# Hash-bucketed attention and two expert layers on one core: turned tiles leave PSUM as an fp16 pair

## The chip, the cores and the metric

One core of a Trainium2 chip. The metric is the device time of one launch in microseconds. Before the change: median 802.08 us of 3 runs (801.53 to 806.88).

## What is computed

Attention for 2 batches, 8 heads, 768 positions and head size 64, in which a query sees only the keys that fall in its own bucket (six sign bits of a projection), then two feed-forward layers on the 1536 x 512 result:

```python
mask = q_bucket[:, :, :, None] == k_bucket[:, :, None, :]
scores = scale * np.matmul(q, k.transpose(0, 1, 3, 2))
scores = np.where(mask, scores, -1000000000.0)
attn = np.exp(scores - np.max(scores, axis=-1, keepdims=True))
attn = attn / (np.sum(attn, axis=-1, keepdims=True) + 1e-09)
x = np.matmul(attn, v)            # then regrouped to (1536, 512)
h = x @ w_in;  x = (h / (1 + np.exp(-h))) @ w_out
h = x @ w_in2; x = (h - np.tanh(h)) @ w_out2
```

## The kernel before

The attention works on tiles of 128 queries against all 768 keys of a head: 6 tiles for each of 16 heads, 96 in all, numbered i. Tiles 0 to 47 are the first batch. For each tile, `scores` (L237) makes the masked scores in PSUM (tile `ps`, two buffers in the first batch), `soft_max` (L248) copies them to SBUF on VectorE and takes the row maximum (L257), `soft_exp` (L261) takes the exponential in place on ScalarE. The product with V needs the weights with keys on the partitions, and there are two ways to turn them:

- Even tiles of the first batch and all of the second: ScalarE rounds to fp16 (`soft_hi`, L299), GpSimd takes the remainder in fp16 (`soft_lo`, L306), and a transposing DMA on SyncE's queue (L308) brings both into a tile `pt`, of which the pool has four buffers. `pv` (L311) then makes 18 products of 128x65: for each of 6 key blocks rounded weights times rounded V (L325), rounded weights times V's remainder (L326), and weights' remainder times rounded V (L327). Column 64 of V is one, so that column 64 of the result is the row sum.
- Odd tiles of the first batch ("direct", L273; here called turned tiles, 24 of them): `turn_p` (L276) transposes on TensorE in fp32 (L285, three blocks for each of two PSUM banks `psm`), copies one bank out on ScalarE (L290) and the other on VectorE (L288) into the spare half of the tile's own SBUF buffer, and `pv` makes 6 fp32 products with V as it was loaded (L321). The row sums come from an accumulator of the exponential (L269), and `denom` takes them up in an operation of its own (L336).

`psm` has three buffers in the first batch; hashes (L172), transposes and the expert layers share them. V of a batch is loaded to `vr` (L194, a buffer that has a single copy and is later used by an accumulator of the expert layers), its row maxima are taken on VectorE (L202), and `prep_v2` writes it as `v16` (ScalarE, L232) and `v16l` (VectorE, L233).

The loop over steps s issues scores of tile s, the turn or the transposing DMA of tile s-2 and the product of tile s-6. Between the batches stand 13 steps without scores. The weights of the expert layers are converted from step 33 on, and from step 61 the expert products (L547 into the hidden layer, L571 out of it) are mixed with the second batch's attention; some 430 us of expert products alone follow. The code's order is not the order of the program: a scheduler reorders the instructions of each engine by priorities and by when it expects buffers free, and each engine then executes its own list in order.

Of the kernel before, what the change touches and what calls it, by code (L numbers as in the profile page):

```python
# [7 lines left out]
F32 = mybir.dt.float32  # L8
F32R = mybir.dt.float32r
F16 = mybir.dt.float16  # L10
I32 = mybir.dt.int32
ACTF = mybir.ActivationFunctionType
ALU = mybir.AluOpType
# [5 lines left out]
PSC = 2.0 ** 11  # L19
# [30 lines left out]
def lsh_attention_moe_kernel(  # L50
# [12 lines left out]
    nc = tc.nc  # L63
    B, H, _, _, S = qkT.shape
    DM, NT = outT.shape
    KD = DM // 128
    D = DM // H
    DFF = w_out1.shape[0]
    NQ = S // 128
    HS = S // 2  # L70
# [8 lines left out]
    sm = ctx.enter_context(tc.tile_pool(name="sm", bufs=4))  # L79
# [24 lines left out]
    def bank():  # L104
        turn[0] += 1
        pool = ps_more[0] if ps_more and turn[0] % ps_turn[1] < ps_turn[0] else ps_m
        return pool.tile([128, 512], F32, tag="m", name="psm")


    def attention(pools, vraw, extra, xw):  # L110
# [6 lines left out]
        xa = [x.rearrange("p a b -> p (a b)") for x in xa]  # L117
        xset = (xa[0][:, 0:S], xa[0][:, S:2 * S], xa[1][:, 0:S], xa[1][:, S:2 * S])

        hlx, vf, vmxs = {}, {}, {}  # L120
        raw, ops, vv, pso, sums, xt, hilo, ptile, pexp, pss, dens = {}, {}, {}, {}, {}, {}, {}, {}, {}, {}, {}

        def load_qk(n):
            b, h = divmod(n, H)
# [66 lines left out]
        def load_v(b):  # L191
            vr = vraw.tile([128, NQ, DM], F32, tag="acc", name="vr")
            for t in range(0, NQ, 2):
                nc.sync.dma_start(out=vr[:, t:t + 2, :],  # L194
                                  in_=v[b, t * 128:(t + 2) * 128].rearrange("(t p) d -> p t d", p=128))
            return vr
# [31 lines left out]
        @early  # L228
        def prep_v2(b, vr, t):
            v16, v16l, vsc = vv[b]  # L230
            src = vr[:, t, :].rearrange("p (h d) -> p h d", h=H)
            nc.scalar.activation(out=v16[:, t, :, 0:D], in_=src, func=ACTF.Copy, scale=vsc)  # L232
            nc.vector.scalar_tensor_tensor(v16l[:, t, :, 0:D], src, vsc, v16[:, t, :, 0:D],  # L233
                                           op0=ALU.mult, op1=ALU.subtract)
            vf[b] = vr

        def scores(i):  # L237
            n, t = divmod(i, NQ)
# [22 lines left out]
        def soft_exp(i):  # L261
            n, t = divmod(i, NQ)
            p, m = pexp[i]
            bi = sm.tile([128, 1], F32, tag="bi", name="bi")
            nc.scalar.activation(out=bi, in_=m, func=ACTF.Copy, scale=-0.125, bias=LN_PSC)
            if direct(i):
                if n not in sums:
                    sums[n] = sm.tile([128, NQ], F32, tag="sums", name="sums")
                nc.scalar.activation(out=p, in_=p, func=ACTF.Exp, scale=0.125, bias=bi, accum_out=sums[n][:, t:t + 1])  # L269
                return  # L270
            nc.scalar.activation(out=p, in_=p, func=ACTF.Exp, scale=0.125, bias=bi)  # L271

        def direct(i):  # L273
            return i < H * NQ and i % 2 == 1

        def turn_p(i):  # L276
            p, _ = pexp.pop(i)
            pt = hlx.pop(i) if i in hlx else wk.tile([128, 2, S], F16, tag="hl", name="ptf")
            pt = pt.rearrange("p a s -> p (a s)").bitcast(F32).rearrange("p (a q) -> p a q", a=NQ)
            w = NQ // 2  # L280
            for u in range(2):
                ps = bank()
                for x in range(w):
                    kt = u * w + x
                    nc.tensor.transpose(ps[:, x * 128:(x + 1) * 128], p[:, kt * 128:(kt + 1) * 128], ident)  # L285
                dst = pt[:, u * w:(u + 1) * w, :].rearrange("p a q -> p (a q)")
                if u:
                    nc.vector.tensor_copy(dst, ps[:, 0:HS])  # L288
                else:
                    nc.scalar.copy(dst, ps[:, 0:HS])  # L290
            ptile[i] = pt

        def soft_hi(i):
# [17 lines left out]
        def pv(i):  # L311
            n, t = divmod(i, NQ)
            b, h = divmod(n, H)
            v16, v16l, _ = vv[b]
            pt = ptile.pop(i)
            if t == 0:
                pso[n] = ps_v.tile([128, NQ, D + 1], F32, tag="o", name="pso")
            o = pso[n][:, t, :]
            if direct(i):
                for kt in range(NQ):  # L320
                    nc.tensor.matmul(out=o[:, 0:D], lhsT=pt[:, kt, :], rhs=vf[b][:, kt, h * D:(h + 1) * D],  # L321
                                     start=(kt == 0), stop=(kt == NQ - 1))
                return
            for kt in range(NQ):
                nc.tensor.matmul(out=o, lhsT=pt[:, kt, :], rhs=v16[:, kt, h, :], start=(kt == 0), stop=False)  # L325
                nc.tensor.matmul(out=o, lhsT=pt[:, kt, :], rhs=v16l[:, kt, h, :], start=False, stop=False)  # L326
                nc.tensor.matmul(out=o, lhsT=pt[:, NQ + kt, :], rhs=v16[:, kt, h, :], start=False,  # L327
                                 stop=(kt == NQ - 1))

        def denom(n):  # L330
            vsc = vv[n // H][2]
            den = sm.tile([128, NQ], F32, tag="den", name="den")
            c = 2 if n < H else 1
            nc.vector.tensor_scalar(den[:, 0:NQ:c], pso[n][:, 0:NQ:c, D], 1e-9 * PSC, vsc, op0=ALU.add, op1=ALU.mult)
            if c > 1:
                nc.vector.tensor_scalar(den[:, 1:NQ:2], sums.pop(n)[:, 1:NQ:2], 1e-9 * PSC, None, op0=ALU.add)  # L336
            nc.vector.reciprocal(den, den)
            dens[n] = den

# [43 lines left out]
        vr = load_v(0)  # L383
# [4 lines left out]
        def at(s):  # L388
            b, r = divmod(s, per + gap)
            return b * per + r if s >= 0 and b < B and r < per else None  # L390

        for s in range(B * (per + gap)):
            evs, late = late, []
            i, i1, i2, j, j1, j3 = (at(s - x) for x in (0, 1, 2, LAG, LAG + 1, LAG + 2))
# [4 lines left out]
            if i2 is not None and direct(i2):  # L399
                turn_p(i2)  # L400
# [5 lines left out]
            if j is not None:  # L406
                pv(j)
# [3 lines left out]
            if i is not None:  # L411
                n, t = divmod(i, NQ)
# [4 lines left out]
            if i is not None:  # L417
                soft_exp(i)
            if j is not None and j % NQ == NQ - 1:
                denom(j // NQ)  # L420
            late += [e2 for e2 in [e() for e in evs] if e2 is not None]
            if i is not None:
                if i % per < 2:
                    for u in range(3):
                        prep_vm(n // H, vr, 3 * (i % per) + u)
                if i % per == 1:
                    prep_v0(n // H, vr)
                    prep_v1(n // H, vr)
                if 2 <= i % per < 4:
                    for u in range(3):  # L430
                        prep_v2(n // H, vr, 3 * (i % per - 2) + u)
                if prep[0] < NHEAD and prep[0] <= limit(n):
                    if prep[1] == 0:
                        split_a(prep[0])
                    elif prep[1] == 1:
                        split_b(prep[0])
                    prep[1] += 1
                    if prep[1] == 3:
                        prep[:] = [prep[0] + 1, 0]
                while nextr < NHEAD and nextr <= (limit(n) + 1 if n < H - 1 else n + (2 if t >= 3 else 1)):  # L440
                    load_qk(nextr)
                    nextr += 1
                if n + 1 < NHEAD:
                    if (n + 1) % H == 0 and t == 0:
                        vr = load_v((n + 1) // H)
# [206 lines left out]
    with ExitStack() as es:  # L652
# [5 lines left out]
        ps_s2 = [es2.enter_context(tc.tile_pool(name="ps_s2", bufs=1, space=PSUM))]  # L658
        pools.append(ps_s2)
        attn = attention(pools, pB[5], pB[3], pB[0])  # L660
        half = NTL // 2 + LAG + GAP
        pre = None
# [87 lines left out]
```

## Time and profile before

| | |
|---|---|
| median of 3 runs | 802.08 us |
| the profiled execution | 797.22 us |
| its span (first to last instruction) | 795.4 us |
| TensorE busy | 744.3 us, 94% |
| VectorE busy | 539.5 us, 68% |
| ScalarE busy | 430.7 us, 54% |
| GpSimd busy | 308.2 us, 39% |
| mean granted TensorE clock | 0.981 |

PE is TensorE, PEld its weight load, DVE VectorE, ACT ScalarE, POOL GpSimd, SP SyncE; a q behind the name means the engine's queue of DMA and control instructions. "Idle before" is the time that the engine stood still just ahead of an instruction, and the arrow names what ended it. Durations of neighbouring instructions overlap at their ends, so an engine's throughput is read from start to start. The granted clock is a share of 2.4 GHz; 0.5 is 1.2 GHz.

### The profile page before, as it was taken

The numbers are of one execution on the slowest core, as the hardware profiler recorded it, in microseconds if no ns is written. First come the engines' busy times: TensorE is split into PE (matmuls) and PEld (weight loads), VectorE is DVE, ScalarE is ACT, GpSimd is POOL, SyncE is SP. The second block draws the span as 40 slices with busy tenths as digits, with TensorE's granted clock in tenths as the row PEclk, the third lists the DMA queues.
The fourth block names the chain that finished last, engine by engine and source line by source line (L and its number), as shares of the span: only waits on it lengthen the run. The fifth ranks groups of instructions, "written<-read, shape, count | busy, mean of one in ns | idle before, by whom it ended". The sixth has DMA issues, their size and how long they took to land.

```text
span 795.4 us, 14025 instructions
## 1 busy us (share of the span) xinstructions
PE 744.3 (94%) x5348; PEld 717.6 (90%) x5348; DVE 539.5 (68%) x1013; ACT 430.7 (54%) x821; POOL 308.2 (39%) x214
## 2 busy tenths in 40 slices
PE   4799997789999998897999999999999999999998
PEld 3789986779988888797999999999999999999998
DVE  6768789698768868777452543998658576584342
ACT  4768878677778769747353441653424334252130
POOL 4455646555766757656355420223011110111000
PEclk8699999989999999999999999999999999999999
DMA  7676587779998996984233320234122220210102
GB/s 256 140 131 131 126 188 194 187 199 191 239 219 204 227 235 136 252 208 140 80 107 106 96 91 1 81 105 130 40 70 60 73 79 30 80 53 1 50 30 80
DMA packets 138878, 100.38 MB, mean 126 GB/s; under 512 B 115870, under 2 KB 118174, under 8 KB 138810
## 3 DMA queue, kind: packets, MB, share of 16 engines
q1 hardware_dynamic: 137712, 97.54, 48.9%
q10 hardware_dynamic: 1098, 1.94, 1.0%
q8 instruction: 42, 0.69, 0.4%
q14 instruction: 26, 0.21, 0.1%
HBM read 57.95 MB, written 11.53 MB: 87 GB/s over the span
## 4 chain that ended last, share of the span: by engine, by line
PE 64%; DMA 7%; ACT 2%; issue 2%; DVE 2%; POOL 1%; SPq 0%; POOLq 0%; ACTq 0%; DVEq 0%
PE psm L571 32%; PE psm L547 29%; DMA pt<-hl 6%; PE ps L244 2%; DMA w<-in_w_out_dram 1%; PE pso L325 1%; POOL hl L306 1%; ACT p L271 1%; PE psm L172 0%; PE pso L327 0%; PE pso L326 0%; DVE cv L525 0%; POOL wl L516 0%; ACT hl L299 0%; ACT cv L523 0%
## 5 line engine op out<-in xcount | busy, mean ns | idle before, releaser
L547 PE MATMUL psm<-xh,wh 128*128 128x384 f32 x512 | 174.9, 342 | 2.1 <-DVE gl L559 1.8
L547 PE MATMUL psm<-xl,wh 128*128 128x384 f32 x512 | 172.9, 338 | 2.1 <-DVE xl L359 2.1
L516 POOL TENSOR_TENSOR wl<-wa,wh 128x512 fp32r<-128x512 f32 x64 | 83.5, 1305 | 232.1 <-ACT wh L515 232.0
L571 PE MATMUL psm<-gh,wh 128*128 128x384 f32 x512 | 172.1, 337 | 0.2 <-DVE gl L559 0.2
L547 PE MATMUL psm<-xh,wl 128*128 128x384 f32 x512 | 171.5, 337 | 0.0
L571 PE MATMUL psm<-gl,wh 128*128 128x384 f32 x512 | 171.2, 334 | 0.0
L571 PE MATMUL psm<-gh,wl 128*128 128x384 f32 x512 | 169.4, 335 | 0.0
L306 POOL TENSOR_TENSOR hl<-p,hl 128x768 f16<-128x768 f32 x72 | 119.8, 1665 | 98.4 <-ACT hl L299 90.7
L257 DVE TENSOR_SCALAR_CACHE_REDUCE p<-ps 128x768 f32<-128x768 f32 x96 | 90.8, 952 | 29.8 <-PE ps L244 24.6
L547 PEld LDWEIGHTS psm<-xh,wh 128*128 128x128 f32 x512 | 97.0, 189 | 2.5 <-DVE gl L559 2.0
L547 PEld LDWEIGHTS psm<-xl,wh 128*128 128x128 f32 x512 | 96.9, 189 | 2.6 <-DVE xl L359 2.6
L244 PE MATMUL ps<-k,q 128*128 128x384 f32 x336 | 82.0, 368 | 17.0 <-DVE p L257 13.8
L547 PEld LDWEIGHTS psm<-xh,wl 128*128 128x128 f32 x512 | 96.7, 189 | 0.1
L571 PEld LDWEIGHTS psm<-gh,wh 128*128 128x128 f32 x512 | 96.1, 188 | 0.6 <-DVE gl L559 0.6
L583 DVE TENSOR_TENSOR acc<-acc,psm 128x384 f32<-128x384 f32 x96 | 52.0, 551 | 65.2 <-PE psm L571 64.6
L571 PEld LDWEIGHTS psm<-gl,wh 128*128 128x128 f32 x512 | 96.2, 188 | 0.0
L571 PEld LDWEIGHTS psm<-gh,wl 128*128 128x128 f32 x512 | 95.8, 188 | 0.0
L559 DVE TENSOR_TENSOR gl<-psm,gh 128x384 fp32r<-128x384 f32 x128 | 70.6, 554 | 29.6 <-ACT gh L558 29.5
L558 ACT CAST gh<-psm 128x384 fp32r<-128x384 f32 x128 | 61.1, 479 | 50.9 <-DVE psm L557 34.4
L244 PEld LDWEIGHTS ps<-k,q 128*128 128x128 f32 x336 | 59.8, 199 | 21.6 <-DVE p L257 17.2
L515 ACT CAST wh<-wa 128x512 fp32r<-128x512 f32 x64 | 39.5, 617 | 60.0 <-DVE wa L514 59.5
L556 ACT ACTIVATE th<-psm 128x384 f32<-128x384 f32 x64 | 31.5, 492 | 71.9 <-PE psm L547 71.7
(99 smaller groups left out, 1298.2 us busy)
## 6 DMA issues: line engine op xcount, KB each, us to landing
w<-in_w_in_dram SPq DMA_DIRECT2D x32, 512.0 KB
w<-in_w_out_dram SPq DMA_DIRECT2D x32, 512.0 KB
r<-in_qkT_dram SPq DMA_DIRECT2D x15, 768.0 KB
wi<-wa SPq DMA_DIRECT2D x16, 256.0 KB
wo<-wa SPq DMA_DIRECT2D x16, 256.0 KB
w<-wi SPq DMA_DIRECT2D x16, 256.0 KB
w<-wo SPq DMA_DIRECT2D x16, 256.0 KB
vr<-in_v_dram SPq DMA_DIRECT2D x6, 512.0 KB
```

What stands on the lines that cost most here:

```text
L244: nc.tensor.matmul(out=ps[:, u, 0:HS], lhsT=a[:, t * 128:(t + 1) * 128], rhs=c[:, u * HS:(u + 1) * HS], start=(j == 0), stop=(j == 1))
L257: nc.vector.tensor_scalar(p.rearrange("p (c s) -> p c s", c=2), pss.pop(i)[:, :, 0:HS], FLOOR, None, op0=ALU.max, op1=ALU.max, accum_out=m)
L271: nc.scalar.activation(out=p, in_=p, func=ACTF.Exp, scale=0.125, bias=bi)
L306: nc.gpsimd.tensor_tensor(hl[:, 1, :], p, hl[:, 0, :], op=ALU.subtract)
L515: nc.scalar.copy(hh, s)
L516: nc.gpsimd.tensor_tensor(ll, s, hh.bitcast(F32), op=ALU.subtract)
L547: nc.tensor.matmul(out=ps, lhsT=a[:, k, fs], rhs=b_[blk][:, k, :], start=(k == 0 and j == 0), stop=(k == KD - 1 and j == 2))
L556: nc.scalar.activation(out=th, in_=ps, func=ACTF.Tanh)
L558: nc.scalar.copy(gh[:, f, :], ps)
L559: nc.vector.tensor_tensor(gl[:, f, :], ps, gh[:, f, :].bitcast(F32), op=ALU.subtract)
L571: nc.tensor.matmul(out=ps, lhsT=a[:, f, ds], rhs=b_[:, f, :], start=(f == 0 and j == 0), stop=(f == F - 1 and j == 2))
L583: nc.vector.tensor_tensor(ac, ac, ps, op=ALU.add)
```

## The change

Turned tiles stay turned on TensorE, but leave PSUM as the DMA's tiles arrive: rounded to fp16 by ScalarE (both banks), with the remainder taken by VectorE from the same bank into the same `pt` tile, which now comes from the pool of four. All tiles take the 18 fp16 products; the fp32 product, the accumulated sums and the reference to `vr` behind `prep_v2` go.

```diff
         def soft_exp(i):
...
-            if direct(i):
-                if n not in sums:
-                    sums[n] = sm.tile([128, NQ], F32, tag="sums", name="sums")
-                nc.scalar.activation(out=p, in_=p, func=ACTF.Exp, scale=0.125, bias=bi, accum_out=sums[n][:, t:t + 1])
-                return
             nc.scalar.activation(out=p, in_=p, func=ACTF.Exp, scale=0.125, bias=bi)
...
         def turn_p(i):
             p, _ = pexp.pop(i)
-            pt = hlx.pop(i) if i in hlx else wk.tile([128, 2, S], F16, tag="hl", name="ptf")
-            pt = pt.rearrange("p a s -> p (a s)").bitcast(F32).rearrange("p (a q) -> p a q", a=NQ)
+            pt = pt_p.tile([128, 2 * NQ, 128], F16, tag="pt", name="pt")
...
-                dst = pt[:, u * w:(u + 1) * w, :].rearrange("p a q -> p (a q)")
-                if u:
-                    nc.vector.tensor_copy(dst, ps[:, 0:HS])
-                else:
-                    nc.scalar.copy(dst, ps[:, 0:HS])
+                hi, lo = (pt[:, x + u * w:x + (u + 1) * w, :].rearrange("p a q -> p (a q)") for x in (0, NQ))
+                nc.scalar.copy(hi, ps[:, 0:HS])
+                nc.vector.tensor_tensor(lo, ps[:, 0:HS], hi, op=ALU.subtract)
             ptile[i] = pt
...
         def pv(i):
...
-            if direct(i):
-                for kt in range(NQ):
-                    nc.tensor.matmul(out=o[:, 0:D], lhsT=pt[:, kt, :], rhs=vf[b][:, kt, h * D:(h + 1) * D],
-                                     start=(kt == 0), stop=(kt == NQ - 1))
-                return
...
         def denom(n):
...
-            c = 2 if n < H else 1
-            nc.vector.tensor_scalar(den[:, 0:NQ:c], pso[n][:, 0:NQ:c, D], 1e-9 * PSC, vsc, op0=ALU.add, op1=ALU.mult)
-            if c > 1:
-                nc.vector.tensor_scalar(den[:, 1:NQ:2], sums.pop(n)[:, 1:NQ:2], 1e-9 * PSC, None, op0=ALU.add)
+            nc.vector.tensor_scalar(den, pso[n][:, :, D], 1e-9 * PSC, vsc, op0=ALU.add, op1=ALU.mult)
```

The lines move: the transposes of `turn_p` are L278 in the changed kernel, its cast L280, its subtraction L281, the scores L243, the row maximum of the softmax L256, the transposing DMA L299, the three products L311, L312 and L313.

The scheduler's order changes with it in three places.

SyncE's list, from the sixth row on, before and then after. `vr` is the fp32 slab of V, `r` the q and k of a head, `hl` the pair of an even tile:

```order
L134 DMA r<-in_qkT_dram 128x1536
L308 DMA_TRANSPOSE pt<-hl 128x12x128 x3
L134 DMA r<-in_qkT_dram 128x1536
L308 DMA_TRANSPOSE pt<-hl 128x12x128 x3
L134 DMA r<-in_qkT_dram 128x1536
L308 DMA_TRANSPOSE pt<-hl 128x12x128 x4
```

```order
L194 DMA vr<-in_v_dram 128x2x512 x3
L134 DMA r<-in_qkT_dram 128x1536
L299 DMA_TRANSPOSE pt<-hl 128x12x128 x3
L134 DMA r<-in_qkT_dram 128x1536
L299 DMA_TRANSPOSE pt<-hl 128x12x128 x3
L134 DMA r<-in_qkT_dram 128x1536
```

The load of the second batch's V, which stood behind the 24th transpose of the list, stands behind the second.

VectorE's list behind the preparation of the first batch's V, before and then after:

```order
L257 TENSOR_SCALAR p,mx<-ps 128x768 x2
L288 COPY p<-psm 128x384
L336 TENSOR_SCALAR den<-sums 128x3
L288 COPY p<-psm 128x384
L257 TENSOR_SCALAR p,mx<-ps 128x768 x2
L185 TENSOR_SCALAR hb<-psm,cst_sb 82x384 x2
```

```order
L281 TENSOR_TENSOR pt<-psm,pt 128x384 x2
L256 TENSOR_SCALAR p,mx<-ps 128x768
L202 TENSOR_REDUCE vm<-vr 128x1 x2
L281 TENSOR_TENSOR pt<-psm,pt 128x384
L256 TENSOR_SCALAR p,mx<-ps 128x768
L202 TENSOR_REDUCE vm<-vr 128x1 x2
L281 TENSOR_TENSOR pt<-psm,pt 128x384 x2
L202 TENSOR_REDUCE vm<-vr 128x1 x2
L256 TENSOR_SCALAR p,mx<-ps 128x768
```

Where single copies stood there are pairs of subtractions, and the row maxima of the second batch's V stand among the first batch's seventh to ninth softmax.

TensorE's list around the last scores of the first batch (`ps_1884` before, `ps_2176` after), before and then after. The names `pt` with a number are tiles of turned weights, `p` with a number the weights ahead of the turn:

```order
L244 MATMUL ps_1884<-k1_1255,q1_1253 128x384 x2
L244 MATMUL ps_1884<-k2_1256,q2_1254 128x384 x2
L351 MATMUL psm_1761<-cst_sb_69,xt_1474 128x128 x3
L172 MATMUL psm_1802<-q1_1721,hw_128 82x384
L172 MATMUL psm_1802<-k1_1723,hw_128 82x384
L172 MATMUL psm_1802<-q2_1722,hw_128 82x384
```

```order
L243 MATMUL ps_2176<-k1_1432,q1_1430 128x384 x2
L243 MATMUL ps_2176<-k2_1433,q2_1431 128x384 x2
L243 MATMUL ps_2373<-k1_1986,q1_1984 128x384 x2
L278 MATMUL psm_1917<-cst_sb_69,p_1841 128x128 x3
L278 MATMUL psm_2002<-cst_sb_69,p_1923 128x128 x3
L278 MATMUL psm_2008<-cst_sb_69,p_1923 128x128 x3
L311 LDWEIGHTS pt_1813
```

Behind these scores eight tiles' products are still to come in the list before, and twelve in the list after; in the middle of the batch scores stand six to seven tiles ahead of the products before, and seven to twelve after.

## Rows read from the trace of the kernel before

**Rows 1.** Groups by line: names, shapes, count | busy us, mean ns | idle before.

```profile
L321 PE MATMUL pso<-vr,p 128*128 128x64 f32 x264 | 35.0, 281 | 0.0
...
L336 DVE TENSOR_SCALAR den<-sums 128x3 f32<-128x3 f32 x8 | 5.3, 659 | 1.0 <-ACT p L269 1.0
L269 ACT ACTIVATION_READ_ACCUMULATOR p<-p,bi 128x1 f32 x24 | 4.5, 188 | 0.0
...
L356 ACT CAST xh<-psm 128x384 fp32r<-128x384 f32 x8 | 3.7, 471 | 0.0
...
L321 PE MATMUL pso<-vr,ptf 128*128 128x64 f32 x24 | 3.0, 274 | 0.0
```

**Rows 2.** Busy time by stage: stretch, PE, PEld, DVE, ACT, POOL, granted clock, DMA share, GB/s.

```profile
60.00:100.00 40.00, 39.82 (x417) 37.64 (x418) 32.07 (x66) 34.29 (x71) 23.99 (x14) 1.00 0.59 129
100.00:139.00 39.00, 32.72 (x321) 29.93 (x320) 33.56 (x64) 31.25 (x63) 21.34 (x13) 0.96 0.78 192
20.00:139.00 119.00, 106.72 (x1008) 98.58 (x1006) 93.80 (x182) 93.59 (x187) 65.75 (x39) 0.93 0.68 152
139.00:153.00 14.00, 12.89 (x138) 12.15 (x137) 8.06 (x19) 9.11 (x18) 7.69 (x8) 1.00 0.63 148
153.00:190.00 37.00, 30.08 (x231) 26.31 (x231) 32.98 (x67) 29.63 (x55) 20.72 (x14) 0.91 0.88 218
190.00:364.00 174.00, 157.99 (x1499) 146.12 (x1497) 132.65 (x260) 126.46 (x222) 111.67 (x73) 1.00 0.95 213
364.00:795.00 431.00, 427.83 (x2454) 427.39 (x2454) 259.37 (x466) 163.10 (x328) 93.43 (x75) 1.00 0.23 70
...
20.00:40.00 20.00, 15.76 (x100) 14.06 (x99) 15.87 (x28) 14.71 (x28) 9.99 (x6) 0.69 0.65 139
120.00:140.00 20.00, 15.52 (x139) 14.00 (x139) 17.82 (x32) 17.26 (x37) 13.85 (x9) 0.91 0.72 186
140.00:160.00 20.00, 15.16 (x146) 13.34 (x144) 13.74 (x30) 13.80 (x24) 11.10 (x9) 0.97 0.71 191
```

**Rows 3.** Timeline of TensorE, 65 to 68 us: start, us, instruction.

```profile
65.92 0.20 PE L325 MATMUL pso<-v,pt 128*128 128x65 f16 x1
...
66.47 1.53 PE L321 MATMUL pso<-vr,p 128*128 128x64 f32 x12
67.84 0.19 PE L325 MATMUL pso<-v,pt 128*128 128x65 f16 x1
```

**Rows 4.** Timeline of ScalarE at 66 us.

```profile
66.22 0.46 ACT L290 COPY p<-psm 128x384 f32<-128x384 f32 x1
66.58 0.84 ACT L299 CAST hl<-p 128x768 f16<-128x768 f32 x1
```

**Rows 5.** Timeline of VectorE, 155 to 162 us.

```profile
155.94 1.28 DVE L202 TENSOR_REDUCE vm<-vr 128x1 f32<-128x512 f32 x2 [0.79 <-DMA vr<-in_v_dram]
...
158.01 1.28 DVE L202 TENSOR_REDUCE vm<-vr 128x1 f32<-128x512 f32 x2
...
159.79 1.27 DVE L202 TENSOR_REDUCE vm<-vr 128x1 f32<-128x512 f32 x2
160.98 1.02 DVE L359 TENSOR_TENSOR xl<-psm,xh 128x384 fp32r<-128x384 f32 x2
161.91 0.95 DVE L257 TENSOR_SCALAR_CACHE_REDUCE p<-ps 128x768 f32<-128x768 f32 x1
```

**Rows 6.** Timeline of TensorE, 150 to 162 us; in brackets its idle time before.

```profile
150.19 0.20 PE L325 MATMUL pso<-v,pt 128*128 128x65 f16 x1 [1.11 <-DMA pt<-hl]
...
161.59 0.69 PE L547 MATMUL psm<-xl,wh 128*128 128x384 f32 x1 [2.07 <-DVE xl L359]
```

**Rows 7.** Timeline of SyncE's queue at 146 us.

```profile
146.49 1.51 SPq L308 DMA_TRANSPOSE pt<-hl  x1
```

**Rows 8.** The chain that ended last: start, us, what.

```profile
180.84 7.62 DMA pt<-hl
...
284.71 9.51 DMA pt<-hl
```

More of the change, by code (lines that the diff above doesn't have):

```diff
@@ L118, in attention @@
         xset = (xa[0][:, 0:S], xa[0][:, S:2 * S], xa[1][:, 0:S], xa[1][:, S:2 * S])
-        hlx, vf, vmxs = {}, {}, {}
-        raw, ops, vv, pso, sums, xt, hilo, ptile, pexp, pss, dens = {}, {}, {}, {}, {}, {}, {}, {}, {}, {}, {}
+        hlx, vmxs = {}, {}
+        raw, ops, vv, pso, xt, hilo, ptile, pexp, pss, dens = {}, {}, {}, {}, {}, {}, {}, {}, {}, {}
         def load_qk(n):
@@ L234, in prep_v2 @@
                                            op0=ALU.mult, op1=ALU.subtract)
-            vf[b] = vr
         def scores(i):
```

## Prediction

> **What bounds the kernel now.** I read the table of stages first, then the groups by line, then the timelines of TensorE, VectorE and SyncE at the places the change touches, and last the chain of waits. The profiled execution took 797.22 us (a span of 795.4 and 1.8 around it); the median shown is 802.08, so the sum below is made on 797.22 and carried over as a share.
>
> The change lies in the attention of the first batch, roughly the stretch from 20 to 153 us, and it frees a load that now falls just behind it. In 20 to 139, where that batch's scores are taken, TensorE is busy 106.72 of 119 us, VectorE 93.80 and ScalarE 93.59; in 139 to 153, the drain of its last value products, 12.89, 8.06 and 9.11 of 14 [rows 2]. Together that is 119.6 us of TensorE in 133, or 0.90, against 101.9 and 102.7. So TensorE is the fullest engine, but not by much. The reader is to see two more things there. From 60 to 100 it is TensorE alone (39.82 of 40). From 100 to 139, where the expert weights begin to be converted beside the attention, VectorE has 33.56 of 39 and TensorE 32.72. Behind 364 only expert products run, and TensorE is busy 427.83 of 431: nothing there can move except by starting earlier or later.
>
> **The change part by part.** There are 24 turned tiles in the first batch (i odd, below 48).
>
> *The value product.* Before, a turned tile takes six fp32 products at L321, which the trace shows as 12 records each; the groups add up to 264 and 24 [rows 1]. At full clock the 12 records start at 66.47 and the next product starts at 67.84: 1.37 us. The 18 fp16 records ahead of them start at 65.92: 0.55 us [rows 3]. The change puts the second in place of the first: 24 x 0.82 = 19.7 us less of TensorE, so 99.9 in that stretch.
>
> *Leaving PSUM.* Before, one half-tile is copied by ScalarE and one by VectorE. Now ScalarE casts both halves to fp16 and VectorE subtracts both. Copies on ScalarE start 0.36 us apart from what follows (66.22 to 66.58) [rows 4], a cast from PSUM of that size lasts as long (471 ns by its group [rows 1]); so ScalarE gets 24 x 0.36 = 8.6 us, less 24 accumulator reads of 188 ns (4.5 us, [rows 1]), and 106.8 in all. Two subtractions of this form on VectorE take 0.93 us (160.98 to 161.91) [rows 5], 0.47 each; one copy goes, two subtractions come, so 24 x 0.47 = 11.3 us. The eight operations on the sums at L336 go (5.3 us [rows 1]); the denominators' other operation takes six columns for three, which I cost at nothing, beside a VectorE sum of over 100 us. The remainder needs the rounded part, so a half-tile's bank is held for both operations in turn, and TensorE waits for the second where it waited for one.
>
> *The load of V.* The fp32 slab of V was read by L321 until the last turned tile; now only prep_v2 reads it. The second batch's load of V therefore moves on SyncE from behind the last fp32 product to behind the second transpose, and its six row maxima on VectorE from the start of the second batch to the first's seventh softmax, as the order shows. They take 1.28 + 1.28 + 1.27 us at 155.94 to 161.06 [rows 5]; that 4 us goes into the first stretch. VectorE there: 101.9 + 11.3 - 5.3 + 4.1 = 112.0 us. The three DMAs are queued ahead of a q/k load and the third transpose on SyncE, and the maxima ahead of three softmaxes on VectorE; if the slab lands late they all wait. TensorE is busy 15.76 of 20 there at a granted 0.69 [rows 2], so up to about 4 us of that is free; I charge nothing more.
>
> *The sum of the first stretch.* The fullest engine is now VectorE with 112.0, with ScalarE 106.8 and TensorE 99.9 beside it. How full can it get? TensorE got 0.90 of the stage; VectorE got 0.86 from 100 to 139 and 0.80 from 60 to 100 [rows 2]. At 0.90 the stage takes 124.5 us (8.5 less), at 0.80 140 (7 more). I take 0.86, since those are the rows in which VectorE is the fullest engine: 130.2, or 2.8 us less.
>
> *Behind it.* VectorE did the three pairs of maxima between 155.94 and 161.06, right ahead of the remainder of x at 160.98; the expert product that needs it waited 2.07 us, till 161.59 [rows 5, 6]. TensorE is busy 30.08 of 37 us from 153 to 190 [rows 2], so the gain lies between nothing and 6.9 us; I take 3.0, near the 3.8 us taken off VectorE. Later stages keep their work; their order changes a little, and from 190 to 364 TensorE has 16 us idle that can go either way by some 4 us.
>
> Sum: -2.8 - 3.0 = -5.8 us, 797.2 to 791.4, or -0.73%; on the median 802.08 that is **796.2 us**. Most of the 19.7 us is lost again: the stage ends with VectorE where TensorE ended it.
>
> **A rule that speaks against the change.** With 99.9 of 130 us, TensorE would be as loosely filled as in 120 to 140 and 140 to 160, where it was busy 15.52 and 15.16 of 20; the granted clock there was 0.91 and 0.97, mostly its upper level (2.4 GHz) with stretches of the lower (1.2) [rows 2]. The Trainium skill, TensorE: Matmul & The Clock Gate, section "HAM oscillation — how this bites in real kernels", says that products which come in bursts with waits between them lose the upper clock again and again. By that rule more of the stretch would run at 1.2 GHz than these rows show, and the last rival below has its price; by the rows nothing is added.
>
> **The rivals.**
>
> *The drain and the stage stay tight.* VectorE reaches the 0.90 that TensorE had, and the whole idle time from 153 to 190 goes: -8.5 - 6.9 = -15.4 us, 786.7 on the median. For it: the scores now run further ahead of the products, as the order shows, so VectorE seldom has nothing to take. Against it: no row shows VectorE above 0.89 (32.98 of 37) for as long.
>
> *The pt buffers decide (slower).* All 48 tiles now share four pt buffers that 24 had, so a transpose by DMA or a cast may begin only when the product four tiles earlier is done. The order shows what that does: twelve products are left when the last score of the batch is issued, where eight were. With four buffers twelve products are three rounds, and I price a round at the landing of a transpose and three products of 0.55 us. A transpose in the first batch was issued at 146.49 and its product started at 150.19 after a wait for it: 3.7 us [rows 6, 7], and the drain takes 16 us, as the sum above has room for. In the second batch transposes on the chain took 7.62 and 9.51 us [rows 8]. At 9.51 the drain takes 33.5 us, 17.4 more: 802.08 - 5.8 + 17.4, about 813.7. The gain is gone from a landing time of 5.6 us on, and slower by 1% from 8.3. For it: DMA share in the first batch 0.59 to 0.78, and a load added. Against it: the wait at 150.19 was 1.11 us, and from 60 to 100 TensorE waited for next to nothing [rows 2, 6].
>
> *The clock.* If the first stretch ran at a granted 0.69, as from 20 to 40 [rows 2], in place of 0.93, TensorE's 99.9 us become 134.6 and it is the bound again: 149.6 at 0.90, 16.6 more than before, less the 3.0 behind it: about 815.7. Against it are the two rows of the same fill, 0.91 and 0.97.
>
> **How the numbers follow.** About 1% is what a measurement of this kernel can tell from no change. Forecast 0.42 (its own range 790 to 803; most of it within 1%, 0.03 beyond at either side), tight stage 0.38, pt buffers 0.15 (at 7.62 us it would still be within 1%, so 0.04 of it), clock 0.05. Faster by over 1% (below 794.1): 0.37 + 0.03 = 0.40. Within 1%: 0.36 + 0.01 + 0.04 + 0.01 = 0.42. Slower: 0.03 + 0.11 + 0.04 = 0.18. The range reaches from the tight stage, 785, to 811, which leaves out the far end of the two slower cases.
>
> **What the next profile would show.** Right: 576 records at each of the three fp16 product lines (six for each of 96 tiles) and none in fp32; 48 casts near 0.47 us and 48 subtractions near 0.55; the maxima of the second batch before 60 us; VectorE at about 112 us in a first stretch of about 130; the first expert products some 5 to 6 us earlier. Wrong: a first stretch of 125 or less (the tight stage), long waits of the products for DMA pt in the drain (the buffers), a granted clock well below 0.9 there, or TensorE records from 190 to 364 with other idle time than 16 us, which the sum holds constant.

## The result and the profile after

The changed kernel takes 791.38 us (median of 4 runs, 789.84 to 792.62) against 802.24: a ratio of 0.9857, interval 0.982 to 0.9894. A second set gave 792.17 us and 0.9871 (0.9844 to 0.9898). So it is faster by 1.3 to 1.4%, some 11 us, where 5.8 us were forecast; the time lies inside the range.

The profile of after, by stage (columns as in [rows 2]):

```profile
20.00:139.00 119.00, 97.21 (x1103) 83.54 (x1101) 93.02 (x193) 93.60 (x180) 64.97 (x38) 0.92 0.72 149
139.00:153.00 14.00, 10.13 (x123) 8.94 (x124) 11.75 (x22) 9.20 (x18) 5.36 (x4) 0.76 0.98 242
153.00:190.00 37.00, 32.38 (x302) 30.00 (x301) 34.30 (x66) 31.50 (x60) 21.97 (x16) 0.95 0.71 164
190.00:364.00 174.00, 165.41 (x1525) 151.48 (x1524) 138.62 (x273) 131.92 (x235) 116.27 (x77) 0.99 1.01 219
364.00:795.00 431.00, 419.88 (x2422) 418.97 (x2420) 254.07 (x455) 158.08 (x318) 91.97 (x72) 1.00 0.22 70
```

Against [rows 2] the first stretch has 9.5 us less of TensorE in the same 119 us: the work went, and idle time came in its place. VectorE, which was to reach 112 us in 130, has 104.8 in 133. The surprise is in 190 to 364, which the sum held constant: TensorE is busy 165.41 of 174 where it was 157.99.

The page's busy line of after, and the groups by line that answer to [rows 1]:

```profile
PE 733.6 (93%) x5492; PEld 700.0 (89%) x5492; DVE 544.4 (69%) x1029; ACT 433.1 (55%) x821; POOL 309.5 (39%) x214
```

```profile
L311 PE MATMUL pso<-v,pt 128*128 128x65 f16 x576 | 70.9, 200 | 15.4 <-DMA pt<-hl 15.3
...
L281 DVE TENSOR_TENSOR pt<-psm,pt 128x384 f16<-128x384 f32 x48 | 25.3, 548 | 4.7 <-ACT pt L280 4.6
...
L280 ACT CAST pt<-psm 128x384 f16<-128x384 f32 x48 | 21.9, 475 | 17.1 <-PE psm L278 15.8 <-PE pso L313 0.8 <-issue 0.3
```

The change does what it says: 576 records at each fp16 line, 48 casts of 475 ns, 48 subtractions of 548 ns.

To place the gain I use one measure for every trace: the **work left** at a time, which is TensorE's busy time in stretches of 2 us times their granted clock, summed from there to the end. Two kernels with the same work left at 190 us are equally far. What the rest takes beyond it is the **loss behind 190** (idle time and lower clock).

```
work left (us) at         20     60    100    140    190   span   loss behind 190
before                 724.8  695.8  656.0  624.0  584.3  795.4   21.1
before, second trace   724.4  694.6  654.8  623.2  583.6  803.0   29.4
after                  710.4  683.4  652.9  621.6  583.7  789.4   15.7
after, second trace    711.9  684.6  652.4  622.0  585.6  792.6   17.0
late_v                 710.7  680.8  643.7  616.2  580.6  797.8   27.2
own_pt                 709.1  683.3  647.3  619.1  586.5  800.4   23.9
mid_11                 709.9  677.6  645.1  617.1  573.0  781.3   18.3
mid_11, second trace   710.3  677.9  644.3  615.8  571.7  779.1   17.4
mid_23                 713.2  680.5  646.4  618.3  575.8  778.6   12.8
mid_35                 714.7  681.7  644.8  620.4  584.3  794.5   20.2
max_held               708.0  677.7  645.7  617.2  585.1  801.9   26.8
mid_11_every4          703.5  675.4  648.1  623.1  591.5  794.7   13.2
double_sub             715.1  692.8  656.0  629.0  593.3  800.3   17.0
```

The measure is good to some 3 us: the ten traces from after on that have the same TensorE instructions (all but mid_11_every4) are equally far at 20 us and give 708.0 to 715.1 there. So the main readings are also made **by records**: the records still to come, each at its median step from start to start (177 ns for scores, 173 for expert products, 112 for fp32 transposes and fp32 value products, 29 for fp16 value products). That gives 608.9 and 608.5 us left at 140 us before and 607.7 and 607.1 after, and at 190 us 572.5 and 572.1 before and 571.9 and 573.4 after.

At 20 us the change has 13.4 us less ahead of it (means of two traces; 19.7 by records). At 190 us nothing is left of that, by either count, and the whole measured gain arises behind 190, where both kernels have the same instructions to execute. Two things are to be explained: who took those 13 to 20 us, and why the rest loses less. The names after the first four are the experiments below.

### The profile page after: what moved, and what is told of

Its sections match the earlier page's. It is cut to its first block, busy times and chain, and to the rows that moved or that the text cites. A ratio compares the mean times of both kernels' runs of the same rounds, so it can differ in the third digit from the quotient of the medians.

```text
span 789.4 us, 14334 instructions
## 1 busy us (share of the span) xinstructions
PE 733.6 (93%) x5492; PEld 700.0 (89%) x5492; DVE 544.4 (69%) x1029; ACT 433.1 (55%) x821; POOL 309.5 (39%) x214
## 4 chain that ended last, share of the span: by engine, by line
PE 55%; DMA 2%; ACT 1%; DVE 0%; issue 0%; POOL 0%; ACTq 0%; DVEq 0%
PE psm L554 28%; PE psm L530 26%; DMA pt<-hl 1%; DMA w<-wi 1%; PE ps L243 0%; ACT xh L577 0%; ACT p L265 0%; POOL hl L297 0%; PE pso L311 0%; POOL wl L485 0%; ACT wh L484 0%; ACT th L536 0%; PE pso L312 0%; PE pso L313 0%; ACT hl L290 0%
## 5 line engine op out<-in xcount | busy, mean ns | idle before, releaser
L256 DVE TENSOR_SCALAR_CACHE_REDUCE p<-ps 128x768 f32<-128x768 f32 x96 | 90.8, 952 | 29.7 <-PE ps L243 20.0
L243 PE MATMUL ps<-k,q 128*128 128x384 f32 x336 | 82.9, 372 | 15.9 <-DVE p L256 9.0
L265 ACT ACTIVATE p<-p,bi 128x768 f32<-128x768 f32 x96 | 89.0, 939 | 2.9
L311 PE MATMUL pso<-v,pt 128*128 128x65 f16 x576 | 70.9, 200 | 15.4 <-DMA pt<-hl 15.3
L311 PEld LDWEIGHTS <-pt 128*128 128x128 f16 x576 | 55.3, 101 | 27.2 <-DMA pt<-hl 17.4
```

The lines of the kernel that those rows point to most:

```text
L243: nc.tensor.matmul(out=ps[:, u, 0:HS], lhsT=a[:, t * 128:(t + 1) * 128], rhs=c[:, u * HS:(u + 1) * HS], start=(j == 0), stop=(j == 1))
L256: nc.vector.tensor_scalar(p.rearrange("p (c s) -> p c s", c=2), pss.pop(i)[:, :, 0:HS], FLOOR, None, op0=ALU.max, op1=ALU.max, accum_out=m)
```

## The experiments

**The two kernels again.**

> The kernel before, unchanged, for a second trace: its first profiled execution took 797.22 us where the timed runs took 801.5 to 806.9. Expected ratio 1.00. If the 4 to 5 us come and go between executions, this trace is longer than 797 in one stretch, and that stretch says which part of the measured gain of 10.9 us the two profiles (797.22 and 791.22, 6.0 apart) don't show. If the trace is again at 797, the profile itself makes the kernel faster.

> The changed kernel, unchanged, for a second trace and a tighter interval: ratio 0.984 to 0.988, 790 to 792 us. Every theory expects the same; if TensorE's idle time behind 190 us is again near 14 us where the kernel before had 19.6, the gain behind 190 is no accident of one execution.

Before: 804.74 us (ratio 0.9997, 0.9967 to 1.0026), its trace 803.0 us long. The execution that the forecast was made on (797.22 us) is below every timed run of this kernel (the lowest of three sets is 797.54). Its second trace is level with it to about 1 us up to 190 us, and loses 8 us behind:

```profile
190.00:364.00 174.00, 159.52 (x1455) 147.90 (x1454) 129.38 (x253) 122.04 (x211) 108.89 (x70) 0.97 0.96 203
364.00:795.00 431.00, 426.93 (x2472) 426.48 (x2472) 260.39 (x468) 167.31 (x337) 95.66 (x76) 0.99 0.24 72
```

The granted clock is 0.97 and 0.99 where [rows 2] have 1.00: more of the stretch ran at the lower level. After: 792.17 us, loss 17.0 again, so the smaller loss is no accident of one execution.

**late_v: the load of V put back.** One column of the first batch's V is read behind the last product, so the load stands behind the 24th transpose as before. In this kernel TensorE's list of the second batch keeps, all through, the distances of the list before (scores three to six tiles ahead of products, behind the first few tiles equally many expert products between them).

```diff
             vv[b] = (v16, v16l, vsc)
+            if b == 0:
+                held.append(vr)
...
+            if i == H * NQ - 1:
+                junk = sm.tile([128, 1], F32, tag="junk", name="junk")
+                nc.vector.tensor_tensor(junk, o[:, 0:1], held.pop()[:, NQ - 1, 0:1], op=ALU.add)
```

> The changed kernel, but the first batch's V slab is read once more behind the last product of the batch (one VectorE operation on one column), so that the load of the second batch's V and its six row maxima stand again behind the 24th transpose. Theory 'early V pays': the maxima fall again right ahead of the first expert products and the kernel loses what the transition gained, 3 to 7 us: 794 to 798. Theory 'early V collides': the load in the first stretch lengthened three transposes to 13 us and TensorE waited 3.4 us for one of them; without it the first stretch is 3 to 5 us shorter and the net is 788 to 792. Rival (V does nothing either way): 791, and all of the gain is the value product's.

800.0 us, ratio 0.9953 (0.9921 to 0.9984), above the range of every theory. Each of the first two has the right sign in its own stretch. Up to 100 us the kernel is 9 us ahead of after (643.7 against 652.9 and 652.4), so the early load, or what comes with it, does collide. At 190 us 3 to 5 us of that are left, and behind 190 it loses them and more. The timelines of TensorE show the transition, last product of the first batch and first of the second, in late_v and in after:

```profile
145.47 0.19 PE L316 MATMUL pso<-v,pt 128*128 128x65 f16 x1
...
170.21 0.20 PE L314 MATMUL pso<-v,pt 128*128 128x65 f16 x1
```

```profile
155.58 0.19 PE L313 MATMUL pso<-v,pt 128*128 128x65 f16 x1
...
168.90 0.20 PE L311 MATMUL pso<-v,pt 128*128 128x65 f16 x1
```

24.7 us with the late load, 13.3 with the early one (18.8 in before). But in after the last product comes 10 us later than in late_v, and 4 us later than in before (152.01; in the second traces 157.35 against 151.47). The early load shortens the transition and delays its start.

**own_pt: a turned tile's pair in its own buffer.**

```diff
-            pt = pt_p.tile([128, 2 * NQ, 128], F16, tag="pt", name="pt")
+            pt = hlx.pop(i) if i in hlx else wk.tile([128, 2, S], F16, tag="hl", name="ptf")
+            pt = pt.rearrange("p a (c q) -> p (a c) q", q=128)
```

> The changed kernel, but a turned tile's fp16 pair goes into the spare half of its own buffer, as its fp32 copy did before, so that the four pt buffers are shared by the 24 transposed tiles alone. Theory 'pt buffers gate': transposes are issued up to two tiles earlier, the waits for pt (4.5 us from 20 to 139 and 3.9 behind) go, 783 to 787. Rival (the transfers themselves take the time, or VectorE ends the stage): 789 to 793.

801.56 us, 0.9956 (0.9929 to 0.9984): slower than after by 10 us, which neither side expected. The buffers aren't what holds the drain: the last product falls at 156.75. Of the gain, 2.7 us is there at 140 (619.1 left) and gone at 190; the rest is a loss of 23.9 behind 190. V is early here; what differs there is the order of the second batch's list.

**mid_23, mid_11, mid_35: V held to a tile in the middle.** As late_v, with `if i == 23:`, 11 or 35. With 23 and 11 the second batch's list keeps the changed kernel's distances throughout (scores mostly four to six tiles ahead of products); with 35 it is in a third order, nearly that of own_pt.

> The changed kernel with the first batch's V slab read once more behind the product of tile 23, so that the second batch's V is loaded behind the 14th transpose: late enough to leave the three long transposes of 35 to 48 us alone, early enough that the second batch's instructions stand in exactly the order of the changed kernel. Theory 'the early load collides, and the second batch's order pays': the first stretch of the late_v run (some 4 us ahead at 190 us) together with the changed kernel's loss behind 190 us (15.7 and 17.0 us of idle time and lower clock): 785 to 789. Rival 'the load costs as much wherever it falls in the first batch': 790 to 793. Rival 'the order of the second batch does nothing': the loss behind 190 us is over 21 us, 795 or more.

> The same with the read behind the product of tile 11, the load behind the 8th transpose, the second batch's order again the changed kernel's. Theory: like the run with tile 23, 785 to 789; if the collision depends on the early part of the batch (q and k loads, first transposes), nearer to 791.

> The same with the read behind the product of tile 35: the load stands behind the 20th transpose, still in the first batch, but the second batch's TensorE list is now in another order (the one of the own_pt run, whose loss behind 190 us was 24 us). Theory 'the order of the second batch decides behind 190': first stretch as with tile 23, loss behind 190 of 22 to 26 us, so 793 to 798. Rival 'it is enough that V is there early': 785 to 790.

mid_23: 785.09 us, 0.9771 (0.973 to 0.9812). mid_11: 776.31 us, 0.969 (0.9648 to 0.9731), better than expected. mid_35: 801.75 us, 0.9974 (0.9947 to 1.0002), though the load is well inside the first batch. The gain with 11 and 23 comes up to 190 us (573 and 576 left, against 584 to 586); behind it they lose what after loses. The time with 35 is above what either side expected: the stretch from 140 to 190 us is slower again (620.4 to 584.3 left), and the loss is 20.2, just under what the theory of the order expected and well over after's. The transition of mid_11:

```profile
143.76 0.19 PE L316 MATMUL pso<-v,pt 128*128 128x65 f16 x1
...
157.05 0.20 PE L314 MATMUL pso<-v,pt 128*128 128x65 f16 x1
```

13.3 us, as in after, from a start 12 us earlier.

**mid_11_again.**

> The kernel with V held behind the product of tile 11 once more, for a second trace and a tighter interval: ratio 0.963 to 0.977, and again 571 to 575 us of TensorE's work left at 190 us. If the first result (776 us) was a lucky set of runs, it comes out with the tile 23 run at 785.

780.74 us, 0.9697 (0.9654 to 0.9741), 571.7 left at 190. This version beats both kernels, by 3.0% and 1.8%.

**max_held: V early, its maxima late.** This parts the transfer from VectorE's share of it.

```diff
+            if i == 11:
+                vmxs[1] = sm.tile([128, NQ], F32, tag="vm", name="vm")
+                nc.vector.tensor_copy(vmxs[1], o[:, 0:NQ])
...
-            if t == 0:
+            if b not in vmxs:
```

> The changed kernel with the second batch's V loaded as early as the change loads it (near 33 us), but its six row maxima held on VectorE behind the product of tile 11 (a copy of six columns of that product goes first into the tile that the maxima write). Theory 'the maxima collide' (VectorE's list, 36 to 42 us, ahead of the hash signs): the first batch's last product falls near 145 us as with the V held back, and 573 to 577 us of TensorE's work are left at 190 us. Rival 'the transfer collides' (three long transposes behind it): last product near 155, 583 to 586 left. The second batch's list is in the order of the own_pt and mid_35 runs, whose loss behind 190 us was 24 and 20 us in their profiles: if the order decides there, the loss is again 19 to 26 us, so 793 to 800 by the first theory and 802 to 810 by the rival; if it was chance, the loss is 13 to 18.

799.19 us, 0.9936 (0.9905 to 0.9968). The time lies in the first theory's range, but the two signs named beforehand don't decide for it: the last product falls at 151.95, between the two, and 585.1 are left at 190 us, the rival's number. Up to 140 us it is nearer to the theory: 677.7 and 617.2 left at 60 and 140 us against 677.6 and 617.1 in mid_11, though the load is issued up to 33.6 us as in after. By records it is less close: 658.5 and 603.3 left, against 656.9 and 601.9 in mid_11 (656.9 and 600.4 in its second trace) and 662.5 and 607.7 in after (661.6 and 607.1). So by 140 us the place of the maxima makes up two thirds or more of what after loses on mid_11; a share of 1 to 3 us can be the transfer's. Busy time from 40 to 50 us in after, mid_11 and max_held:

```profile
40.00:50.00 10.00, 5.84 (x58) 5.17 (x58) 6.74 (x17) 5.04 (x9) 5.18 (x3) 0.83 1.15 120
```

```profile
40.00:50.00 10.00, 8.53 (x143) 7.66 (x141) 6.74 (x16) 6.27 (x13) 6.45 (x4) 1.00 0.72 158
```

```profile
40.00:50.00 10.00, 6.51 (x103) 5.70 (x102) 5.58 (x14) 6.34 (x13) 6.62 (x4) 1.00 1.05 176
```

(max_held did more just ahead: 687.7 are left at 50, as 687.5 in mid_11, and 692.9 in after.) What after and max_held lose between 140 us and the last product isn't settled by the maxima. The loss behind 190 is 26.8, about as expected for that order.

The place itself, on VectorE, ScalarE and TensorE of after:

```profile
36.34 1.28 DVE L202 TENSOR_REDUCE vm<-vr 128x1 f32<-128x512 f32 x2 [0.90 <-DMA vr<-in_v_dram]
...
39.00 1.28 DVE L202 TENSOR_REDUCE vm<-vr 128x1 f32<-128x512 f32 x2
...
41.12 1.27 DVE L202 TENSOR_REDUCE vm<-vr 128x1 f32<-128x512 f32 x2
...
44.64 0.67 DVE L185 TENSOR_SCALAR hb<-psm,cst_sb 82x384 fp32r<-82x384 f32 x1
...
48.78 0.48 ACT L280 CAST pt<-psm 128x384 f16<-128x384 f32 x1 [4.25 <-PE psm L278]
...
49.70 0.73 ACTq L188 DMA_DIRECT2D l<-hb  x1
...
45.47 0.20 PE L311 MATMUL pso<-v,pt 128*128 128x65 f16 x1 [3.43 <-DMA pt<-hl]
```

and in mid_11:

```profile
40.52 0.67 DVE L186 TENSOR_SCALAR hb<-psm,cst_sb 82x384 fp32r<-82x384 f32 x1
...
42.01 0.73 ACTq L189 DMA_DIRECT2D l<-hb  x1
```

and in max_held:

```profile
41.94 0.74 ACTq L188 DMA_DIRECT2D l<-hb  x1
...
44.82 0.20 PE L311 MATMUL pso<-v,pt 128*128 128x65 f16 x1 [3.49 <-DMA pt<-hl]
```

The second half of the hash signs (`hb`) is written 4.1 us later in after than in mid_11. The copy of the signs (`l<-hb`) is issued by ScalarE's queue behind a cast that waits for a transpose, which stands on TensorE behind a product that waits for its `pt`: three in-order lists, and the copy goes out at 49.70 where it went at 42.01. The product's own wait isn't the maxima's doing: max_held has it too (3.49 us). In both, the transposes ahead of it hold SyncE's queue longer than in mid_11; in after, max_held and mid_11:

```profile
34.58 13.24 SPq L299 DMA_TRANSPOSE pt<-hl  x3
```

```profile
34.67 12.37 SPq L299 DMA_TRANSPOSE pt<-hl  x3
```

```profile
33.93 8.89 SPq L302 DMA_TRANSPOSE pt<-hl  x3
```

(11.26 us in before, from 34.30, without the load.) What the place of the maxima decides is on which side of that wait the copy goes out: with them held it goes at 41.94, ahead of it. Early maxima without the early transfer were not tried. Three heads on, TensorE waits for another such copy (2.86 us in the second trace of after), and the granted clock is low in the stretch (TensorE at 88.53, then 85 to 90 and 90 to 95):

```profile
88.53 0.98 PE L243 MATMUL ps<-l,h 128*128 128x384 f32 x2 [3.45 <-DMA l<-hb]
```

```profile
85.00:90.00 5.00, 1.55 (x7) 1.34 (x7) 0.79 (x2) 2.69 (x6) 4.25 (x3) 0.69 1.02 142
90.00:95.00 5.00, 5.00 (x57) 4.88 (x56) 2.07 (x5) 3.81 (x8) 2.06 (x2) 0.63 0.07 14
```

From 80 to 100 us after does 13 us of work where before does 20. That the second wait follows from the first was not tried by itself.

**double_sub: VectorE made dearer.** Each subtraction is done twice.

```diff
-                nc.vector.tensor_tensor(lo, ps[:, 0:HS], hi, op=ALU.subtract)
+                for _ in range(2):
+                    nc.vector.tensor_tensor(lo, ps[:, 0:HS], hi, op=ALU.subtract)
```

> The changed kernel with each of the 48 subtractions done twice, 48 x 0.47 = 22.6 us more of VectorE in the first stretch and nothing else. My forecast's theory (VectorE ends the first stretch): the first stretch is longer by 15 to 25 us, 806 to 817. Rival (transfers and latencies end it, VectorE has some 20 us of slack): longer by 3 to 10 us at 190 us, where part is the bank held longer.

803.93 us, 1.0004 (0.9979 to 1.003), 12 us over after. At 140 it is 7.2 us behind after's mean (4.7 by records), at 190 8.7 (593.3 against 584.6; 9 by records), for 22.6 us added. VectorE had slack for some 14 of them; it did not end the stretch. Its stretch, and the wait that grew:

```profile
20.00:139.00 119.00, 94.61 (x1003) 78.90 (x1002) 106.63 (x221) 92.50 (x174) 62.00 (x37) 0.91 0.63 144
```

```profile
PE ps L243 <- DVE p L256: 15.0, 16, 4.5
```

15.0 us against 5.2 in after: with more on VectorE the scores wait for the copy out of `ps`.

**mid_11_every4: fewer turned tiles.** `i % 4 == 1` in place of `i % 2 == 1`, on top of mid_11.

> V held behind the product of tile 11, and only every fourth tile of the first batch turned on TensorE (12 tiles in place of 24; 12 more go through ScalarE's rounding, GpSimd and the transposing DMA). The second batch's list is the changed kernel's. TensorE has 12 x 0.7 = 8.4 us less, VectorE 11.3 us less, the DMA 12 transposes more. If VectorE or TensorE ends the first stretch: 5 to 10 us shorter, 767 to 772. If the transposes and latencies end it (the waits for pt and k): 3 to 12 us longer, 779 to 789.

796.12 us, 0.9889 (0.9849 to 0.993): longer by 15 to 20 us than mid_11, past the far end of the second expectation. It starts with 6.6 us less work and has 19 us more left at 190 (591.5). Its waits from 20 to 139 us (us, times, longest):

```profile
PE pso L314 <- DMA pt<-hl: 9.2, 5, 3.7
...
PE pso L314 <- DMA pt<-p: 3.6, 3, 1.8
```

In mid_11 the wait for `pt<-hl` there is 7.9 us and the second one is absent. Freed TensorE and VectorE time bought nothing: the first stretch does not go by the sum of either engine. That transfers and the lists' waits for one another set it is the reading that is left; these waits explain some 5 of the 19 us, and which took the rest isn't shown.

**The loss behind 190 by order of the second batch.** With the changed kernel's order (after, mid_11, mid_23, mid_11_every4, six traces) it is 12.8 to 18.3 us; with the order before (before, late_v, three traces) 21.1 to 29.4; with the third (own_pt, mid_35, max_held) 20.2 to 26.8; double_sub has a fourth, 17.0. The changed kernel's order stays below the second and third whatever the first batch looks like, and mid_23 and mid_35, which differ in the tile that holds V alone, fall on either side. The wait that differs most from 190 to 364 us is that of the products for `pt`; in before, after, mid_23 and late_v:

```profile
PE pso L325 <- DMA pt<-hl: 11.8, 10, 2.3
```

```profile
PE pso L311 <- DMA pt<-hl: 6.9, 6, 2.7
```

```profile
PE pso L314 <- DMA pt<-hl: 3.8, 6, 1.3
```

```profile
PE pso L314 <- DMA pt<-hl: 13.2, 8, 3.7
```

Over all thirteen traces that wait goes with the order too: 3.8 to 6.9 us with the changed kernel's, 11.8 to 13.2 with the order before, 8.6 to 11.5 with the third, 5.9 in double_sub. No run changed the second batch's list alone, so the order is the cause by this agreement and not by a trial of its own, and what in it matters is open: on average scores stand 4.8 tiles ahead of products in the order before, 5.0 in the changed kernel's.

The scheduler made another list for the second batch because V's load was free to move; that this list is the better one is luck of the scheduler, and nothing here says which rule of its own led to it. Every run with this order has V early, but not the other way round: own_pt, max_held and mid_35 have V early and the third order.

## Why the prediction was right, and where not

The direction and the range held; the sum, -5.8 us, is half of what was measured, and it was reached by steps of which several did not hold. They came out so:

- *The value product*, 19.7 us less of TensorE: right by records (19.7), too large in busy time. The work left at 20 us is 13.4 us less. From start to start, weighted with the clock, the first batch's products went from 44.3 to 28.1 us (16.2); the transposes, which now stand in threes between product records, went the other way, from 15.6 to 17.1.
- *Leaving PSUM*, +11.3 - 5.3 us of VectorE: nearly right. VectorE's busy time went from 539.5 to 544.4 (4.9 more, 6.0 forecast), ScalarE's from 430.7 to 433.1 (2.4 more, 4.1 forecast).
- *VectorE ends the first stretch at 0.86*: this step failed. The 2.8 us forecast were there only on the way: after is 2 us ahead at 140 us (1 by records) and 3 us behind at 152 (615.4 and 615.7 left against 613.1 and 612.3). Nor did VectorE end the stretch: double_sub shows its slack, and max_held beside mid_11 shows what took most of the saving up to 140 us. Moving three pairs of maxima (4 us) ahead of the hash signs put a copy behind a product's wait, through three lists. I had named the queue ("ahead of three softmaxes on VectorE") and charged nothing beyond the 4 us; the price at 140 us is 4 to 6 us (621.8 left against 615.8 to 617.1), and 12 to 15 us at the last product (155.58 and 157.35 against 143.76 and 142.04), of which max_held (151.95) explains only the smaller part; the rest stays open.
- *The transition*, -3.0: near in size (from 152 to 190 us after does 2 us more work than before), but it made up for a late start. From last product to first it went from 18.8 to 13.3 us, while the last product, forecast earlier, came 4 to 6 us later; at 190 us the two kernels are level.
- *Behind 190 nothing changes*: failed. TensorE's idle time and lower clock there fell from 25 to 16 us (means of two traces). I had left 4 us either way for the order, and did not ask what the order before lost.
- *The rivals.* The buffers: own_pt speaks against them; the wait for `pt` in the drain was 3.9 us once. The clock: 0.92 granted from 20 to 139 us, not 0.69; but in the drain from 139 to 153 it was 0.76 and 0.74 in the two traces of after, where both of before have 1.00, and no term of the sum had that. The tight stage: its 786.7 was reached only with V held, and with VectorE near the forecast's filling and not at 0.90: busy 112.4 of 133 us in mid_23 (785.1 us), 0.84, and 116.5 in mid_11 (776 and 781 us), 0.88.

Two errors of opposite sign thus stand behind the sum: the first 190 us gave 6 us less than it held, the rest some 9 more. That the time fell inside the range is therefore luck: what the sum counted on was gone by 190 us, and the gain that was measured stands in the stretch that it held constant.

## What to carry to other kernels

When a change frees a buffer, follow what the scheduler does with the freedom: here the place of one load and six small reductions, with the list that the scheduler then made for the second batch, decided some 20 us (776 and 781 to 802), as much as the products that the change was about, and one dependency that holds them back to the product of tile 11 (mid_11) was worth as much again as the change. Count an instruction that is moved ahead in an in-order list at its chain (who stands behind it on its engine, and whose queue that one's DMA is issued from), not at its duration. And compare traces by work left at fixed times: equal busy shares hid that the whole gain lay in a stretch that the change does not touch.

## What the hardware showed unexpectedly

The same program, level to 1 us at 190 us, lost 21.1 us behind it in one execution and 29.4 in another; the difference is in stretches at the lower clock, 0.97 granted from 190 to 364 where the other had 1.00. In after, the granted clock fell within a wait of 3.45 us on TensorE (0.69 from 85 to 90 us) and was 0.63 over the next 5 us, in which the fp16 product records start 54 ns apart in place of 31. But not every such wait is followed by the lower clock: behind one of 3.43 us at 45.47 the granted clock from 40 to 50 us is 0.83 in after, and with one of 3.49 at 44.82 it is 1.00 in max_held.
